# 16 products of zeros ahead of the first sums in place of 21

## The chip, the core and the metric

One core of one Trainium2 chip. The metric is the device time of one execution in microseconds; the time of a kernel is the median of its runs. Five engines work side by side, each through its own instructions in order: TensorE (PE; its weight loads are listed apart as PEld), VectorE (DVE), ScalarE (ACT), GpSimd (POOL) and SyncE (SP), which here only issues DMAs.

## What is computed

A gated linear recurrence over 768 steps for 4 x 8 heads of width 48, and behind it a two-layer network with the gate h * cos(h):

```python
for t in range(S):
    state = alpha[:, :, t, :, None] * state + np.einsum('bhd,bhe->bhde', k[:, :, t], v[:, :, t])
    y[:, :, t] = np.einsum('bhd,bhde->bhe', q[:, :, t], state)
...
h = x @ w_in
g = h * np.cos(h)
return (g @ w_out).astype(np.float32)
```

x is y with the heads of a step side by side: 3072 rows of 384; w_in is 384 x 2048, w_out 2048 x 384.

## The kernel before

The 3072 rows are cut into 12 pairs J of two blocks of 128 steps. Each pair goes through the same steps:

- `load` (L105, SP's queue): alpha, k, q and v of the pair, 384 KB each. `load_w1` and `load_w2` (L121, L127) bring the weights in four pieces each, issued by POOL.
- `ln` (L141, ACT): logarithms of alpha, tile lna.
- `cums0` and `cums` (sums at L155, decay sums at L167, PE): running sums of the logarithms by products with triangular matrices, tile cums_h for the first three pairs.
- `icp` and `exps` (L192, L200, ACT): exponentials of the sums with both signs, tiles icp and cp.
- `scale_k` (L212) and `scale_q` (L216), on DVE or POOL: kh = k * icp and qh = q * cp. `cast_v` (L219, POOL) makes vp of v, `decay` (L244, POOL) the factors c.
- `outer` (L291, PE): the state's increments U_ps from kh and vp. `stack_v_pe` (L235, PE, pairs 0 to 2) regroups v through vs_ps, and ACT copies it to vs (L239). `trans` (L260, PE) turns kh and qh into T_ps, `evict_T` (L266) copies that to qkT.
- `scores` (L274, PE) gives A_ps, `mask` (L279, DVE) A_sb; `add_state` (L305, L307, DVE) and `decay_state` (L313, POOL) carry the state on as us and un.
- `yT` (L340, PE) gives y_ps, `evict_y` (L350) xT. Then `mlp1` (L359, PE, tile h_ps, four parts a pair), `cosine` (L365, ACT, c_sb), `gate` (L370, DVE, gsb) and `mlp2` (L387, PE, o_ps), whose result `evict_o` (L396) copies out and `store` (L403) writes.

The order is written out by hand. `PLAN` gives a due time in ns for each step of each pair, and the steps are emitted in the order of these numbers; the numbers do not become waits. Each engine then runs its own instructions in that order, and waits only for its data and buffers. Two loads have a further condition: from pair 2 on, alpha is gated behind `yT` of pair 1 on SP's queue (`GATES`, L99), with all that SP issues after it.

`idle(n)` (L407 to L411) puts n products of a 128x128 tile of zeros with a 128x512 tile of zeros on PE. Their result, idle_ps, is never read. Their only input is the tile zeros, which DVE's first instruction sets (L52). `IDLE` (L494) says where they stand among the steps, as pairs of due time and number. The first entry lies ahead of all sums; one product follows the sums of pair 0, eight those of pair 1, and the other four entries lie between the next steps up to 18,254.

Of the kernel before, what the change touches and what calls it, by code (L numbers as in the profile page):

```python
# [16 lines left out]
def kernel(  # L17
# [473 lines left out]
        "out 0": "47770 53670 76970 97327 92197 114044 134921 150722 154222 155552 167028 178835",  # L491
        "out 1": "44770 66136 87674 100827 112274 133721 136121 156752 149522 168228 170958 180161",
    }
    IDLE = [(1501, 21), (7915, 1), (9416, 8), (12569, 4), (14554, 5), (16389, 3), (18254, 3)]  # L494

    order = []
    for key, line in PLAN.items():
        kind, *rest = key.split()
        for J, word in enumerate(line.split()):
            if word != "-":  # L500
                t, _, eng = word.partition(":")
                args = [J] + [int(x) if x.isdigit() else x for x in rest] + [{"A": "ACT", "D": "DVE", "P": "POOL"}[x] for x in eng]
                order.append((int(t), len(order), kind, args))
    for t, n in IDLE:
        order.append((t, len(order), "idle", [n]))
# [34 lines left out]
```

## Time and profile before

| | |
|---|---|
| median of 3 runs | 190.49 us (189.67, 190.49, 190.68) |
| profiled execution | 189.73 us, of which the span from its first to its last instruction is 187.7 us |
| PE busy | 177.2 us, 94% of the span |
| DVE, ACT, POOL busy | 72%, 67%, 41% of the span |
| products of zeros (L411) | 42 listed, 12.7 us busy |
| first sums (L155) | start at 8.03 us |

Times in the profile count from the start of the span. In a timeline a row gives the start, the duration, the engine, the line, the operation, the tiles written and read, and how many such instructions follow one another; what stands in brackets is the idle time of the engine before the row and what ended it. Matmuls overlap, so the distance from one start to the next tells more of PE's pace than the duration of one. Some products are missing from the lists.

### The profile page before, as it was taken

What the parts mean: (1) busy time and instruction counts of PE and PEld (TensorE: products, weight loads), DVE (VectorE), ACT (ScalarE), POOL (GpSimd) and SP (SyncE); (2) the same over time, 40 slices, a digit from 0 to 9 for tenths busy, and PEclk for the clock granted to TensorE, in tenths of its full rate; (3) what the DMA queues carried; (4) which work ended last, traced back from release to release, by engine and by line L of the source; (5) the groups of instructions that cost most, each with busy time, mean ns of one, the idle gap of its engine ahead of it and who ended that gap; (6) DMA issues with size and microseconds to landing.
All of it is one profiled execution on the core that took longest, in us unless ns stands there. A gap on an engine that the chain in (4) does not pass through costs nothing.

```text
span 187.7 us, 5795 instructions
## 1 busy us (share of the span) xinstructions
PE 177.2 (94%) x2471; PEld 126.7 (67%) x2474; DVE 134.3 (72%) x184; ACT 125.3 (67%) x161; POOL 77.4 (41%) x110
## 2 busy tenths in 40 slices
PE   7997799998999999999999999999999999999990
PEld 2444678664577776775688668686776786776880
DVE  7069775589799899589657986885876666573550
ACT  2466876899598977788577999728956182372520
POOL 5059610257664733783894068830540310100000
PEclk9999999999999999999999999999999999999998
DMA  6999999999959988996799943600042005501303
GB/s 152 261 256 154 185 203 236 255 264 265 249 137 302 265 184 217 265 268 166 195 280 259 216 106 90 166 0 3 3 114 73 0 21 124 128 1 45 84 0 84
DMA packets 60537, 29.47 MB, mean 157 GB/s; under 512 B 51424, under 2 KB 60512, under 8 KB 60512
## 3 DMA queue, kind: packets, MB, share of 16 engines
q1 hardware_dynamic: 56640, 25.86, 59.8%
q0 software_dynamic: 3712, 3.15, 11.0%
q8 instruction: 19, 0.31, 0.7%
q10 hardware_dynamic: 160, 0.10, 0.2%
q14 instruction: 6, 0.05, 0.1%
HBM read 25.17 MB, written 4.72 MB: 159 GB/s over the span
## 4 chain that ended last, share of the span: by engine, by line
PE 71%; ACT 16%; DVE 7%; issue 3%; DVEq 0%
PE h_ps L359 31%; PE o_ps L387 23%; PE idle_ps L411 5%; PE y_ps L340 3%; ACT c_sb L365 3%; ACT qkT L266 3%; DVE gsb L370 3%; PE T_ps L260 2%; ACT cp L200 2%; ACT L136 2%; ACT L365 2%; PE A_ps L274 2%; PE U_ps L291 2%; ACT lna L141 2%; ACT icp L192 2%
## 5 line engine op out<-in xcount | busy, mean ns | idle before, releaser
L370 DVE TENSOR_TENSOR gsb<-h_ps,c_sb 128x1024 bf16<-128x1024 f32 x48 | 58.1, 1221 | 22.3 <-ACT c_sb L365 21.5
L365 ACT ACTIVATE c_sb<-h_ps,halfpi 128x1024 bf16<-128x1024 f32 x48 | 53.0, 1113 | 27.4 <-PE h_ps L359 23.4
L359 PE MATMUL h_ps<-xT,w 128*128 128x256 bf16 x576 | 66.7, 273 | 1.4 <-issue 0.6
L387 PE MATMUL o_ps<-w,gsb 128*128 128x384 bf16 x368 | 66.7, 326 | 0.0
L359 PEld LDWEIGHTS <-w 128*128 128x128 bf16 x576 | 55.6, 98 | 10.4 <-issue 1.9
L387 PEld LDWEIGHTS <-gsb 128*128 128x128 bf16 x368 | 33.8, 98 | 21.2 <-DVE gsb L370 0.6
L313 POOL TENSOR_TENSOR un<-us,c 128x384 bf16<-128x384 f32 x20 | 16.8, 843 | 40.3 <-DVE us L305 33.9
L279 DVE TENSOR_TENSOR A_sb<-A_ps,msk 128x1024 bf16<-128x1024 f32 x24 | 28.9, 1216 | 1.3 <-PE A_ps L274 1.3
L212 POOL TENSOR_TENSOR kh<-k,icp 128x384 bf16<-128x384 f32 x17 | 16.9, 999 | 8.7 <-ACT icp L192 8.7
L216 POOL TENSOR_TENSOR qh<-q,cp 128x384 bf16<-128x384 f32 x15 | 15.4, 1032 | 10.9 <-ACT cp L200 10.9
L149 POOL TENSOR_TENSOR a<-a 128x384 f32<-128x384 f32 x9 | 9.3, 1037 | 12.9 <-DMA a<-in_alpha_dram 12.9
L411 PE MATMUL idle_ps<-zeros 128*128 128x512 bf16 x42 | 12.7, 445 | 1.6 <-DVE zeros L52 1.2
L219 POOL CAST vp<-v 128x768 bf16<-128x768 f32 x12 | 9.9, 824 | 9.0 <-DMA v<-in_v_dram 8.9
L141 ACT ACTIVATE lna<-a 128x768 bf16<-128x768 f32 x12 | 10.2, 846 | 4.5 <-DMA a<-in_alpha_dram 4.5
L136 ACT ACT_TABLE_LOAD x9 | 11.5, 1283 | 0.9 <-PEq L524 0.7
L266 ACT COPY qkT<-T_ps 128x1024 bf16<-128x1024 bf16 x8 | 8.0, 1016 | 6.2 <-PE T_ps L260 3.8
L266 DVE COPY qkT<-T_ps 128x1024 bf16<-128x1024 bf16 x16 | 10.8, 682 | 1.3 <-ACT qkT L266 1.3
L365 ACT ACT_TABLE_LOAD x9 | 11.5, 1283 | 0.2
L305 DVE TENSOR_TENSOR us<-U_ps,un 128x384 f32<-128x384 f32 x16 | 8.7, 550 | 3.8 <-PE U_ps L291 2.8
L396 DVE COPY o_sb<-o_ps 128x384 f32<-128x384 f32 x12 | 6.6, 552 | 6.6 <-PE o_ps L387 6.6
L274 PE MATMUL A_ps<-qkT 48*128 48x128 bf16 x192 | 9.2, 218 | 1.0 <-ACT vs L239 0.6
L396 ACT COPY o_sb<-o_ps 128x384 f32<-128x384 f32 x11 | 5.3, 478 | 7.1 <-PE o_ps L387 5.2
(69 smaller groups left out, 155.1 us busy)
## 6 DMA issues: line engine op xcount, KB each, us to landing
k<-in_k_dram SPq DMA_DIRECT2D x12, 384.0 KB, 5.5
a<-in_alpha_dram SPq DMA_DIRECT2D x12, 384.0 KB, 5.9
v<-in_v_dram SPq DMA_DIRECT2D x12, 384.0 KB, 6.2
q<-in_q_dram SPq DMA_DIRECT2D x12, 384.0 KB, 6.0
out_dram<-o_sb SPq DMA_DIRECT2D x46, 96.0 KB, 2.7
vs<-vp SPq DMA_DIRECT2D x36, 64.0 KB, 2.0
w<-in_moe_w_out_dram POOLq DMA_DIRECT2D x4, 384.0 KB, 9.9
w<-in_moe_w_in_dram POOLq DMA_DIRECT2D x4, 384.0 KB, 7.0
```

The costliest lines, as they stand in the source:

```text
L136: nc.scalar.preload_act_table_set("natural_log_exp_and_others")
L141: nc.scalar.activation(out=lna_t[J % NL][:, :, :, 0:D].rearrange("p e h d -> p h e d"), in_=a_sb.pop(J), func=AF.Ln)
L212: eng.tensor_tensor(out=kh_t[J % NQ][:, e, :, 0:D], in0=kqv["k", J][:, :, e], in1=icp_, op=ALU.mult)
L216: eng.tensor_tensor(out=qh_t[J % NQ][:, e, :, 0:D], in0=kqv["q", J][:, :, e], in1=cp, op=ALU.mult)
L266: copy(out=qkT_sb[J][:, c], in_=T_ps[J][:, c].rearrange("r n e s -> r n (e s)"))
L279: nc.vector.tensor_tensor(out=A_sb[J][:, c].rearrange("s a p t -> s (a p) t"), in0=A_ps.pop((J, c)).rearrange("s a p t -> s (a p) t"), in1 ...
L313: nc.gpsimd.tensor_tensor(out=u, in0=U_sum.pop(n), in1=c2_sb[J][:, :, c].unsqueeze(3).to_broadcast([C, NP, 2, D]), op=ALU.mult)
L359: nc.tensor.matmul(h_ps[J, u][:, f, :], w1[:, kk, ft * C : (ft + 1) * C], xT[J][:, kk, :], start=(kk == 0), stop=(kk == KT - 1))
L365: nc.scalar.activation(out=c_sb[J, u], in_=h_ps[J, u], func=AF.Sin, bias=halfpi, scale=1.0)
L370: nc.vector.tensor_tensor(out=gsb[J][:, u * FW : (u + 1) * FW], in0=h_ps.pop((J, u)), in1=c_sb.pop((J, u)), op=ALU.mult)
L387: nc.tensor.matmul(o_ps[J, c][:, 0:DM], gsb[J][:, ft, c * C : (c + 1) * C], w2[:, ft], start=(ft == 0), stop=(ft == NF - 1))
L411: nc.tensor.matmul(idle_ps[0], zeros[:, 0:C], zeros, start=True, stop=True)
```

## The change

The first entry of `IDLE` holds 16 in place of 21. Its place among the steps stays, and no other step is touched.

```diff
-    IDLE = [(1501, 21), (7915, 1), (9416, 8), (12569, 4), (14554, 5), (16389, 3), (18254, 3)]
+    IDLE = [(1501, 16), (7915, 1), (9416, 8), (12569, 4), (14554, 5), (16389, 3), (18254, 3)]
```

On PE five pairs of a weight load and a product go; the order of all else, on PE and on the other engines, is the same.

## Prediction

> **What bounds the kernel now.** I read the page first, then the chain that ended last in order of time, then the timelines of the first 24 us, because the change touches only there.
>
> The page:
>
> ```profile
> span 187.7 us, 5795 instructions
> ...
> PE 177.2 (94%) x2471; PEld 126.7 (67%) x2474; DVE 134.3 (72%) x184; ACT 125.3 (67%) x161; POOL 77.4 (41%) x110
> ```
>
> PE is busy 94% of the span, so what PE starts earlier at the front may be kept to the end, if nothing stops it on the way. The chain, in order of time (start, us, what), says whether the front is PE's:
>
> ```profile
> 1.20 7.00 PE idle_ps L411 x21
> 8.19 0.65 PE cums_h L155 x4
> 8.84 0.18 PE cums_h L167 x8
> 9.02 0.24 PE idle_ps L411
> 9.26 0.65 PE cums_h L155 x4
> 9.91 0.19 PE cums_h L167 x8
> ...
> 11.03 1.10 DVE kh L212 x2
> ...
> 12.18 0.47 PE U_ps L291 x14
> 12.65 0.30 PE vs_ps L235 x4
> 12.95 0.97 PE idle_ps L411 x4
> 13.92 0.59 PE T_ps L260 x32
> ```
>
> The 21 products of zeros head the chain, and the chain never leaves the instructions behind them: sums of pair 0, sums of pair 1, ACT's exponentials, DVE's kh, then PE again. What did the first sums need? ACT's timeline:
>
> ```profile
> 5.86 0.84 ACT L141 ACTIVATE lna<-a 128x768 bf16<-128x768 f32 x1 [3.83 <-DMA a<-in_alpha_dram]
> 7.36 0.84 ACT L141 ACTIVATE lna<-a 128x768 bf16<-128x768 f32 x1 [0.67 <-DMA a<-in_alpha_dram]
> 9.06 0.49 ACT L192 ACTIVATE icp<-cums_h 128x384 f32<-128x384 f32 x1 [0.85 <-PE cums_h L167]
> ```
>
> The logarithms of pair 0 end at 6.70 (5.86 + 0.84), those of pair 1 at 8.20. PE starts the first sums only at 8.03 (PE's timeline), 1.33 us after their input: the zeros, not the data, hold them. ACT then stands idle 0.85 us, from 8.20 to 9.06.
>
> **The change, step by step.** The instruction order differs in five weight loads and five products of zeros on PE; no wait, no DMA and no other engine's order changes.
>
> Step 1, the removed products. PE's weight loads, one for each product, give the spacing:
>
> ```profile
> 5.01 0.15 PEld L411 LDWEIGHTS <-zeros 128*128 128x128 bf16 x1 [0.28 <-issue]
> 5.44 0.15 PEld L411 LDWEIGHTS <-zeros 128*128 128x128 bf16 x1 [0.28 <-issue]
> 5.86 1.84 PEld L411 LDWEIGHTS <-zeros 128*128 128x128 bf16 x9 [0.28 <-issue]
> 7.82 0.10 PEld L155 LDWEIGHTS <-tri 128*128 128x128 bf16 x1
> ```
>
> One product each 0.43 us up to 5.86, then nine loads in 1.84 us: (1.84 - 0.10) / 8 = 0.217 us each. The column of the granted clock says 1.00 all the while; that the array runs at half rate until about 5.9 us is seen in the spacing alone. The five products taken out are behind that point (single starts: the 12th at 5.86, the 17th at 6.95, the 21st at 7.82). So the first sums move from 8.03 to 6.95, by 5 x 0.217 = 1.08 us. Their input is there at 6.70, so nothing new is late.
>
> Step 2, the sums of pair 1. They stood at 9.10, and would go to 8.02. Their logarithms end at 8.20; PE followed such a row by 0.06 us later in the trace (Ln ends 36.84, PE 36.90). They start at about 8.25: **0.85 us** earlier, and 0.23 of the 1.08 are lost to ACT. ACT's first exponential goes from 9.06 to 8.21, so ACT's seven exponentials, which run without a gap from 10.13 on, also move by 0.85.
>
> Step 3, what lies beside them. DVE's kh follows ACT. The k inputs landed at about 4.3 (issue 0.74 + 3.6) and 8.9 (2.87 + 6.0), in time. U_ps also needs the cast of v, and that is tied to a DMA and does not move: it ends at 11.24. The kh that U_ps waits for ended at 12.13 and would end at 11.28. A tie, so no loss by the cast's end; but now DVE's kh run beside it. The timeline of all engines shows what such neighbours did:
>
> ```profile
> 10.42 0.82 POOL L219 CAST vp<-v 128x768 bf16<-128x768 f32 x1 [7.23 <-DMA v<-in_v_dram]
> ...
> 11.03 1.56 DVE L212 TENSOR_TENSOR kh<-k,icp 128x384 bf16<-128x384 f32 x3 [0.89 <-ACT icp L192]
> ...
> 12.96 1.03 DVE L216 TENSOR_TENSOR qh<-q,cp 128x384 bf16<-128x384 f32 x2 [0.37 <-ACT cp L200]
> ...
> 14.37 1.66 DVE L216 TENSOR_TENSOR qh<-q,cp 128x384 bf16<-128x384 f32 x2
> ...
> 14.61 1.01 POOL L313 TENSOR_TENSOR un<-us,c 128x384 bf16<-128x384 f32 x1
> ```
>
> Two qh alone took 1.03 us; two beside POOL's un took 1.66. Taken singly, the second of these took 1.19 in place of 0.55, a loss of 0.64, beside a POOL product that reads two tensors. The only row beside this cast is the first kh, at 11.03: 0.62 in place of 0.55, with 0.21 us in common, a loss of 0.06. After the change some 0.8 us of kh lies beside the cast. The bounds are 0.06 and 0.64; going by the row of the cast itself, 0.06 / 0.21 x 0.82 = 0.23, I take **0.20**. U_ps thus moves by 0.85 - 0.20 = 0.65.
>
> The GPSIMD Engine Reference of the Trainium skill (section Specifications) says that GpSimd shares its SBUF interfaces with VectorE and contends with DVE instructions that have two SBUF inputs, as kh has. The qh rows agree. By that rule alone, with no price, this step costs something; with no contention the sum would be 0.85.
>
> Step 4, behind U_ps. vs_ps, four products of zeros and T_ps follow without a gap on PE, and ACT's copy at 14.54 had waited 1.61 us for T_ps; they move with U_ps. qh of pair 0 would start at 12.11 (12.96 - 0.85); q landed at about 11.8 by the 1.5 us steps of the loads (a at 5.86 and 7.36, the second q at 7.09 + 6.2 = 13.3). Enough. qh of pair 1 goes from 14.37 to 13.52, against 13.3.
>
> Step 5, the weights, which could eat the gain. POOL issues them behind the same exponentials (c at 12.24 waits for ACT), so they are issued earlier too. Even if they landed as before, they would do: the second block of w1 lands at 22.26 (15.56 + 6.7) and is used at 23.7; the third at 24.33 (17.13 + 7.2), used at 25.04; the fourth at 26.8 (17.91 + 8.9), used at 27.49. The smallest slack is 0.69, over the 0.65. The next alpha, gated by yT of pair 1, landed at 34.66 and was used at 36.00. From 28 us on everything waits for PE, ACT or DVE, and moves as a whole.
>
> **The sum**: -1.08 + 0.23 + 0.20 = -0.65 us. Against the profiled execution, 189.73 us (span 187.7 and 2.03 around it), that gives 189.08. The three timed runs have their median at 190.49, 0.76 above the profiled one; taken from the median, **189.84 us**, or -0.34%. About 0.5% (0.95 us) is what a measurement of this kernel can tell from no change.
>
> **The rivals.**
>
> *Late release.* The Trainium skill, TensorE: Matmul & The Clock Gate (Part 1), says that the window which frees the clock runs freely, so that the number of slow products differs from execution to execution. No view here shows a second execution. As a mechanism of this kernel: each product still slow costs 0.43 - 0.22 = 0.21 us more, and 0.76 us, the distance of the median from the profiled run, are 3.6 such products. Then the 21 end at about 8.8 and the 16 at about 7.7; pair 1's logarithms hold nothing back, and the full 1.08 is kept but for some 0.1 beside the cast (kh would start near 10.7, when half of the cast is over). 190.49 - 0.98 = 189.51. For it: the runs differ by 1.0 us. Against: the spread may have other causes. Chance 0.27.
>
> *The cast at its full price.* If a kh beside the cast loses 0.64, as beside un, 0.21 us are left: 190.28. Against it: the cast reads one tensor, and its own row is far cheaper. Chance 0.15.
>
> *Slower: the clock falls back.* With five products fewer, PE has its next hole earlier and larger: the eight products behind pair 1's sums would end at about 10.83, and U_ps starts at 11.5, a hole of some 0.65 us where now there is 0.1 (last zeros issued 11.46, U_ps at 11.77) and then 0.19. If a hole of that size in the weakly filled stretch from 11 us on were enough to halve the rate again, the next release would take as long as the first, 1.20 to 5.86, that is 4.66 us. PE's pieces of the chain in 11.5 to 16.2 are U_ps, vs_ps, zeros and T_ps, 0.47 + 0.30 + 0.97 + 0.59 = 2.33 us, and they double: -0.65 + 2.33 = +1.68, 192.2 us. The point is a hole longer than any seen without harm: PE stood 0.62 us before 16.30 and 0.50 before 22.25, and products of zeros just behind the first still took 0.22. That speaks against it. Chance 0.13.
>
> That the change does not do what it says is excluded by the instruction order.
>
> **Chances and range.** Forecast 0.45, late release 0.27, full price 0.15, clock 0.13. The range 189.0 to 191.0 holds the first three with a spread of half a microsecond in the median, and leaves out the slow clock. Faster by over 0.5% means under 189.54: half of the late release, with the lower edge of the forecast (no contention gives 189.64), and part of the runs' spread: 0.34. Slower by over 0.5% is the clock: 0.13. Within: 0.53.
>
> **What would show it.** Step 1: first sums near 6.95, weight loads of zeros 0.43 apart up to about 5.9. Step 2: pair 1's sums just behind the end of the second Ln, ACT's first exponential at 8.2. Step 3: DVE's kh at about 10.2 and longer than 0.55; U_ps at 11.5. Step 5: first h_ps near 21.6, with no wait for weights. Wrong: products at 0.43 us after 11 us, or h_ps earlier by 0.65 and the span not.

## The result, and the profile after

The changed kernel takes 189.09 us in the median of 10 runs (188.69 to 189.64), the kernel before 190.50 (189.64 to 190.78): a ratio of 0.9939, with a 95% interval of 0.9918 to 0.9961. Two later comparisons of the same two kernels (below) gave 0.9964 (0.9944 to 0.9983) and 0.9954 (0.9933 to 0.9976). The gain is thus some 0.4% to 0.6%, 0.7 to 1.2 us; 0.34% was forecast.

The profiled executions show less of it: 189.54 us against 189.73.

```profile
span 187.5 us, 5788 instructions
...
PE 176.4 (94%) x2469; PEld 126.2 (67%) x2469; DVE 134.8 (72%) x184; ACT 125.3 (67%) x161; POOL 77.8 (42%) x110
```

The first sums and ACT's first exponential start within 0.1 us of the forecast, pair 1's sums 0.16 later. The timeline of all engines of the changed kernel (start, duration, engine, line, operation):

```profile
6.01 0.84 ACT L141 ACTIVATE lna<-a 128x768 bf16<-128x768 f32 x1 [3.99 <-DMA a<-in_alpha_dram]
...
6.91 0.32 PE L155 MATMUL cums_h<-lna,tri 128*128 128x384 bf16 x1 [0.40 <-ACT lna L141]
...
7.52 0.84 ACT L141 ACTIVATE lna<-a 128x768 bf16<-128x768 f32 x1 [0.66 <-DMA a<-in_alpha_dram]
...
8.27 0.47 ACT L192 ACTIVATE icp<-cums_h 128x384 f32<-128x384 f32 x1
8.41 0.32 PE L155 MATMUL cums_h<-lna,tri 128*128 128x384 bf16 x1 [0.28 <-ACT lna L141]
...
10.34 2.14 DVE L212 TENSOR_TENSOR kh<-k,icp 128x384 bf16<-128x384 f32 x3 [1.01 <-ACT icp L192]
10.56 1.02 POOL L219 CAST vp<-v 128x768 bf16<-128x768 f32 x1 [7.38 <-DMA v<-in_v_dram]
```

The first sums start at 6.91, the moment their logarithms are there, those of pair 1 at 8.41 in place of 9.10; ACT no longer waits at 8.3. Then the gain is lost: three kh take 2.14 us in place of 1.56, for the second, which starts at 10.82 inside POOL's cast, takes 1.18 in place of 0.55. The chain of the changed kernel, in order of time, carries the loss on:

```profile
8.41 0.81 PE cums_h L155 x4
9.22 0.19 PE cums_h L167 x8
...
10.34 1.66 DVE kh L212 x2
...
12.05 0.47 PE U_ps L291 x14
...
13.78 0.59 PE T_ps L260 x32
...
22.11 2.79 PE h_ps L359 x24
```

U_ps comes at 12.05 against 12.18, and the first h_ps at 22.11 against 22.25. That is this line of the kernel before:

```profile
22.25 2.79 PE h_ps L359 x24
```

The front, moved by 0.7 us at pair 1's sums, gave 0.14.

Nor was the zeros' pace the same. PE's weight loads of the changed kernel:

```profile
4.16 0.15 PEld L411 LDWEIGHTS <-zeros 128*128 128x128 bf16 x1 [0.27 <-issue]
4.58 1.43 PEld L411 LDWEIGHTS <-zeros 128*128 128x128 bf16 x7 [0.28 <-issue]
6.13 0.10 PEld L155 LDWEIGHTS <-tri 128*128 128x128 bf16 x1
```

The fast spacing begins at 4.58, where before it began at 5.86.

The largest difference between the two traces lies far behind the front. The chain of the kernel before, and then that of the changed one, in the 72 h_ps products of 95 to 104 us:

```profile
95.46 2.84 PE h_ps L359 x25
98.30 0.62 issue
98.92 5.31 PE h_ps L359 x47
```

```profile
95.77 3.38 PE h_ps L359 x30
99.15 0.12 issue
99.27 4.76 PE h_ps L359 x42
```

PE stands 0.62 us behind the 25th product and waits for nothing that the profile shows; with five pairs of instructions fewer it stands 0.12 us behind the 30th. Counted in PE's weight loads and products from the first one, it is the same place, row 2737: the block begins at row 2687 before and at 2677 after (three products of zeros that the list of before lacks are counted in, since their weight loads are listed). The block as a whole takes 8.77 us before and 8.26 after.

### The profile page after: what moved, and what is told of

Its sections match the earlier page's. It is cut to its first block, busy times and chain, and to the rows that moved or that the text cites. A ratio compares the mean times of both kernels' runs of the same rounds, so it can differ in the third digit from the quotient of the medians.

```text
span 187.5 us, 5788 instructions
## 1 busy us (share of the span) xinstructions
PE 176.4 (94%) x2469; PEld 126.2 (67%) x2469; DVE 134.8 (72%) x184; ACT 125.3 (67%) x161; POOL 77.8 (42%) x110
## 4 chain that ended last, share of the span: by engine, by line
PE 57%; ACT 16%; DVE 7%; DMA 6%; POOL 5%; SPq 4%; issue 3%; POOLq 0%; DVEq 0%
PE h_ps L359 25%; PE o_ps L387 20%; ACT c_sb L365 4%; PE y_ps L340 3%; DMA a<-in_alpha_dram 3%; DMA v<-in_v_dram 3%; ACT qkT L266 3%; DVE gsb L370 3%; ACT L136 2%; SPq L225 2%; PE T_ps L260 2%; ACT L365 2%; PE A_ps L274 2%; ACT icp L192 2%; ACT cp L200 2%
## 5 line engine op out<-in xcount | busy, mean ns | idle before, releaser
L411 PE MATMUL idle_ps<-zeros 128*128 128x512 bf16 x40 | 11.5, 431 | 1.2 <-DVE zeros L52 1.2
```

## The experiments

The theory from here on is in two parts. **Front**: the first sums are freed, and how much of that reaches U_ps hangs on the release of the clock and on kh beside the cast. **Refill**: the hole is a wait for PE's next packet of instructions, and five pairs fewer shift where among the h_ps it lies. The rival to each is that the other is all.

This table gathers what the traces show, one profiled execution each, in us: begin of the fast spacing, start of the 14 products of U_ps that wait for the second of two kh, start of the first h_ps, length of the 72 h_ps of 95 to 104 us and the hole in it with the product it follows, and the ratio to the kernel before with its interval.

| kernel | fast from | U_ps | h_ps | block, hole | ratio |
|---|---|---|---|---|---|
| before (21) | 5.86 | 12.18 | 22.25 | 8.77, 0.62 at 25 | |
| changed (16) | 4.58 | 12.05 | 22.11 | 8.26, 0.12 at 30 | 0.9939 (0.9918 to 0.9961) |
| e1, 21 again | 4.98 | 12.21 | 22.26 | 8.73, 0.59 at 25 | 0.9999 (0.9978 to 1.0021) |
| e2, 16 again | 6.29 | 12.00 | 22.05 | 8.19, 0.05 at 30 | 0.9964 (0.9944 to 0.9983) |
| e3, 21, v first | 4.54 | 11.59 | 21.65 | 8.43, 0.29 at 25 | 0.9982 (0.9956 to 1.0008) |
| e4, 16, v first | 6.29 | 11.54 | 21.59 | 7.98, none | 0.9928 (0.9903 to 0.9953) |
| e5, 16 + 5 tiny | 4.16 | 12.12 | 22.17 | 8.32, 0.18 at 25 | 0.9983 (0.9962 to 1.0003) |
| e6, 21, 5 fewer later | 6.66 | 12.46 | 22.60 | 8.00, none | 0.9978 (0.9951 to 1.0004) |
| e7, 26 | 4.97 | 12.72 | 22.85 | 9.49, 1.35 at 20 | 1.0084 (1.0054 to 1.0114) |
| e8, 5 moved | 5.01 | 12.42 | 22.47 | 8.94, 0.80 at 25 | 0.9992 (0.9975 to 1.0009) |
| e9, 11 | 4.07 | 12.11 | 22.16 | 8.71, 0.57 at 35 | 0.9950 (0.9927 to 0.9974) |
| e10, 16 a third time | 6.71 | 12.16 | 22.21 | 8.02, none | 0.9954 (0.9933 to 0.9976) |

**Second profiles of both kernels** (no edit).

> The kernel before, unchanged, for a second profile. Front theory (the gain is made ahead of 22 us, and its size in one execution hangs on when the clock is released and on what DVE's kh meet beside POOL's cast): the release of the clock, seen in the spacing of the zeros' weight loads, lies elsewhere than at 5.9 us, and each slow product more delays the first sums by 0.21 us; with a release 1.5 us later the sums start near 8.8 and the time is near 190.6, with the same release near 189.8. Rival (the gain is made in a later stage): the first h_ps starts near 22.25 whatever the time of the execution, and a slower execution loses its time behind 40 us.

Measured: 190.04 us in the median. The release came 0.9 us earlier, and pair 1's sums with it (strict's weights at 8.64 in place of 9.10). U_ps did not. PE's weight loads of e1, and then its DVE timeline:

```profile
4.98 2.26 PEld L411 LDWEIGHTS <-zeros 128*128 128x128 bf16 x11 [0.24 <-issue]
7.36 0.10 PEld L155 LDWEIGHTS <-tri 128*128 128x128 bf16 x1
```

```profile
10.57 2.06 DVE L212 TENSOR_TENSOR kh<-k,icp 128x384 bf16<-128x384 f32 x3 [0.89 <-ACT icp L192]
```

With 21 products too, an early release puts the kh beside the cast, and three take 2.06 us: U_ps comes at 12.21. That was not expected; it means that with an early release 21 and 16 products reach U_ps within about 0.2 us of each other.

> The changed kernel, unchanged, for a second profile. Front theory: first sums at 6.9 to 7.1; where the second kh takes 0.55 us the first h_ps starts near 21.5 and the time is near 188.8, where it takes 1.18 as in the first profile h_ps starts near 22.1 and the time is near 189.5. Rival: first h_ps near 22.1 in both cases, and the difference arises behind it.

Measured: 189.46 us. The second kh was slow again (three in 2.14 us), and h_ps came at 22.05, as expected for that case. The profiled execution, at 189.22, was 0.3 faster than the first, with h_ps only 0.06 earlier; the rest arose between 78 and 89 us, so the rival's remark on a later stage was right.

**The cast out of the way**: v of pair 0 is loaded ahead of k of pair 1, with 21 products (e3) and with 16 (e4).

```diff
-        "load v": "3750 8250 ...
+        "load v": "2300 8250 ...
```

> 21 products, and v of pair 0 loaded ahead of k of pair 1, so that POOL's cast ends near 9.8, ahead of the kh. Front theory: with 21 products the cast lay hardly beside the kh (0.06 us), so this gives 190.4, within 0.2 of the kernel before. Rival: the order of these two loads does not matter with 21 nor with 16.

Measured: 190.09. As expected in time; in its trace, with an early release, three kh took 1.50 us and h_ps came 0.6 earlier. That execution, at 188.84, was the fastest of the twelve, so its trace does not stand for their median.

> 16 products, and the same exchange of two loads. Front theory: the cast is off the kh, each of the three takes 0.55 us, U_ps starts near 11.5 in every execution, h_ps near 21.5, and the time is 188.8 with less spread, 0.3 to 0.5 below the median of 16 products alone; against 21 products with the same exchange 1.0 to 1.6 us are won. Rival: within 0.2 us of 16 products alone (189.1).

Measured: 188.85, a ratio of 0.9928, as the front theory had it; by the quotient of the two ratios 16 products win 0.5% over 21 here (1.0 us). Less spread was not seen: six runs lie between 188.19 and 189.34. DVE's timeline of e4:

```profile
10.45 1.50 DVE L212 TENSOR_TENSOR kh<-k,icp 128x384 bf16<-128x384 f32 x3 [1.15 <-DMA k<-in_k_dram]
```

The cast ends ahead of them, each takes 0.55 again, and U_ps is 0.5 us ahead of 16 products alone. So in the traces of 16 the front's gain was lost beside the cast, and 0.5 us of it can be had. With v first, k lands later and the kh wait for it, with 21 as with 16: U_ps comes at 11.59 and at 11.54. The 1.0 us is thus not in the front of these two executions: they differ by 0.55 us, of which 0.45 lies in the block of h_ps. What more the medians differ by, no trace shows. By its median, e4 is the fastest kernel here; its interval overlaps that of 16 products alone.

**The refill.** In e5 five products of two columns stand ahead of the first h_ps, so that PE's rows from there on are counted as with 21; in e6 the 21 stay, and five of the eight products behind pair 1's sums go, so that the rows from U_ps on are counted as with 16.

```diff
+            nc.tensor.matmul(idle_ps[0][:, 0:2], zeros[:, 0:C], zeros[:, 0:2], start=True, stop=True)
...
+    order.append((21900, len(order), "tiny", [5]))
```

```diff
-    IDLE = [(1501, 21), (7915, 1), (9416, 8), ...
+    IDLE = [(1501, 21), (7915, 1), (9416, 3), ...
```

> 16 products ahead of the first sums, and five products of two columns of zeros just ahead of the first h_ps, where PE waits 0.5 us for ACT anyway; from there on PE's instructions are counted as with 21. Refill theory (a part of the gain is that PE's next packet of instructions, needed at its row 2737, comes into the h_ps of 95 to 104 us five products later than with 21): the hole behind the 25th of these 72 products is back, 0.3 to 0.6 us, where with 16 it is 0.05 to 0.12 behind the 30th; the time is about 0.5 above 16 products alone, near 189.8. Front theory alone: no hole of its own, the time of 16 products, 189.1 to 189.5.

> 21 products ahead of the first sums, and three in place of eight behind the sums of pair 1, where PE waits for kh anyway; from U_ps on PE's instructions are counted as with 16. Refill theory: front as with 21 (U_ps' second product at 12.2 or later, h_ps at 22.25 or later), but the hole is behind the 30th product of the h_ps of 95 to 104 us and under 0.2 us; the time lies 0.5 below the kernel before, near 189.7. Front theory alone: the time of the kernel before, 190.1, as the sums are where they were. If the clock falls back in the hole ahead of U_ps, slower by over 1 us.

Measured: 189.74 and 189.51. The chain of e5, then that of e6, over the same products:

```profile
95.42 2.83 PE h_ps L359 x25
98.26 0.18 issue
98.44 5.31 PE h_ps L359 x47
```

```profile
95.81 8.00 PE h_ps L359 x72
```

The hole is back at the 25th product with 16 zeros in front, smaller than expected, and gone with 21. So its place hangs on how many instructions precede it and not on the front. Its length hangs on the packet too: in e5 a packet on the queue "q8 instruction" moved at 95.70, in the kernel before at 96.14, with the block at 95.42 and at 95.46. Each of the two kernels has about one half of the gain (0.2% each). Their intervals reach 1, so the times alone do not prove the halves; the traces show that the hole comes and goes with the count. In e6 PE stood 0.82 us ahead of those 14 products of U_ps, longer than any hole of the changed kernel there (0.49), and the next four products of zeros were as fast as before (four weight loads in 0.55 us).

**Five more, and five moved.**

```diff
-    IDLE = [(1501, 21), (7915, 1), ...
+    IDLE = [(1501, 26), (7915, 1), ...
```

> 26 products ahead of the first sums. Front theory: the sums start 1.08 later than with 21 at the same release of the clock; up to a release near 5 us the cast's place beside the kh is left at the same time, so that U_ps moves by 0.4 to 0.5 then, and by 1.08 with a later release: 0.5 to 1.1 slower than the kernel before. Refill theory adds 0.3 to 0.5, as the hole comes behind the 20th product: 0.8 to 1.5 slower in all, 191.0 to 191.6.

Measured: 191.58, a ratio of 1.0084; between the bounds. U_ps came 0.54 later and h_ps 0.60, with an early release, and the hole grew to 1.35 us behind the 20th product. The chain of e7:

```profile
96.07 2.29 PE h_ps L359 x20
98.36 1.35 issue
99.71 5.85 PE h_ps L359 x52
```

```diff
-    IDLE = [(1501, 16), (7915, 1), ...
+    IDLE = [(1501, 16), (7915, 6), ...
```

> 16 products ahead of the sums of pair 0, and the other five moved behind them, ahead of the sums of pair 1. Front theory: the chain goes over pair 1, whose sums start near 9.0 as with 21 and an early release; with a late release they are 0.2 to 0.5 later than with 16. Refill theory: as many instructions as with 21, so the hole of 0.6 us near 98 us is there. Both: 190.0, hardly under the kernel before. If the sums of pair 0 carried the gain: 189.4.

Measured: 189.96, a ratio of 0.9992. Pair 0's sums started as early as with 16 and brought nothing: the front goes over pair 1, and the hole (0.80 us) is back behind the 25th product, as with 21.

**Fewer still, and 16 a third time.**

```diff
-    IDLE = [(1501, 16), ...
+    IDLE = [(1501, 11), ...
```

> 11 products ahead of the first sums, five fewer again. Both theories: the sums wait for the logarithms as with 16, so U_ps stays near 12.0; the hole near 98 us would lie behind the 35th product and is gone, 0 to 0.1 us less than with 16: 189.0 to 189.4. If the clock needs the zeros: they end near 5.5, PE stands until 6.9, and in executions where the clock is not yet released the sums of both pairs take twice as long (0.8 us each in place of 0.4 to 0.5): up to 1 us slower than 16, with more spread.

> The changed kernel a third time, for its ratio beside 11 products on one chip. Front and refill together: 0.4% to 0.6% under the kernel before; first h_ps near 22.1, a hole of 0 to 0.15 us behind the 30th product of the h_ps of 95 to 104 us.

Measured: 188.91 and 189.36, ratios of 0.9950 and 0.9954. Eleven are no better than 16, as the sums wait for the logarithms in both, and U_ps for the cast: in the five executions with 16 or 11 products and v in its old place, U_ps starts 1.49 to 1.51 us behind the start of the cast, which waits for v's load. Nor was the clock lost: in this execution, with 11, PE stood 1.85 us ahead of the first sums, and the four took 0.81 us, as in the first trace with 16:

```profile
6.94 0.32 PE L155 MATMUL cums_h<-lna,tri 128*128 128x384 bf16 x1 [1.85 <-ACT lna L141]
```

The profiled execution of e9 took 191.12 us; the other ten lie at 188.8 to 189.8. It shows a third place that gives and takes: POOL's cast of v that waits for its load near 77 us. That load was issued at 72.49 by SP behind slow issues of regrouping DMAs (4.47 us for four, 3.53 in e2); what follows came 1.1 us later than in the first trace of 16. The packet moved at 98.85, 2.0 us behind the start of the h_ps at 96.87 in place of 0.3 to 0.9 in the other traces, and the hole, 0.57 us behind the 35th product, was there all the same. "Gone" was too much to expect.

## Why the prediction was right, and where it was not

*Steps 1 and 2* held: first sums at 6.91 (forecast 6.95), pair 1's at 8.41 (8.25, with the logarithms themselves 0.16 later), ACT's first exponential at 8.27 (8.21). That the first sums hit 6.95 is luck: with the fast spacing from 4.58 the zeros were through earlier, PE stood 0.40 us, and the logarithms, not the zeros, set the 6.91.

*Step 3* is the term that was mis-sized. The mechanism, kh beside the cast, was named and bounded between 0.06 and 0.64; the value taken was 0.20, and the two kh ahead of U_ps took 1.66 us in place of 1.10, which is 0.56. What failed is the scaling of the loss with the time in common (0.06 / 0.21 x 0.82). The rows show a wait instead. These are single kh of the changed kernel, of e1 and of e8, and behind the last two the cast that each met:

```profile
10.82 1.18 DVE L212 TENSOR_TENSOR kh<-k,icp 128x384 bf16<-128x384 f32 x1
```

```profile
10.57 1.11 DVE L212 TENSOR_TENSOR kh<-k,icp 128x384 bf16<-128x384 f32 x1 [0.89 <-ACT icp L192]
...
10.45 0.82 POOL L219 CAST vp<-v 128x768 bf16<-128x768 f32 x1 [7.26 <-DMA v<-in_v_dram]
```

```profile
11.08 0.82 DVE L212 TENSOR_TENSOR kh<-k,icp 128x384 bf16<-128x384 f32 x1 [1.65 <-ACT icp L192]
...
10.66 0.82 POOL L219 CAST vp<-v 128x768 bf16<-128x768 f32 x1 [7.47 <-DMA v<-in_v_dram]
```

The casts end at 11.58, 11.27 and 11.48, the kh at 12.00, 11.68 and 11.90: each 0.41 to 0.42 behind the cast, however long the two ran side by side. The kernel before fits (11.65 behind 11.24), and so does its second qh behind un (16.03 behind 15.62). So the prediction's two bounds, 0.06 and 0.64, were one behaviour, met late or early in POOL's instruction. It works the other way too: a cast that starts while a kh runs ends 0.68 behind that kh (11.58 behind 10.90 in the changed kernel, 10.13 behind 9.45 in e3), and the kh, having come first, loses nothing (0.56). With 0.56 the step would have left 0.85 - 0.56 = 0.29 at U_ps; the logarithms came 0.16 later in this execution, and 0.13 was measured. The GPSIMD Engine Reference of the Trainium skill (section Specifications) has it that DVE instructions with two SBUF inputs contend with GpSimd. These rows agree; the price is theirs alone.

*Steps 4 and 5* held: T_ps and the copies moved with U_ps, no h_ps waited for weights. The sentence that from 28 us on everything moves as a whole did not. It holds to 78 us, where the changed kernel is 0.14 ahead. At 89 us it is 0.3 behind, since the cast of v at 77 us waited longer for its load; behind the h_ps of 95 to 104 it is 0.20 ahead, for that block takes 0.51 less. The refill was in no term and in no rival, though the hole stood in the page's chain as "issue" and could be found there.

*The rivals.* Late release: the release does differ from execution to execution, from 4.07 to 6.71 us in twelve traces, as the Trainium skill, TensorE: Matmul & The Clock Gate (Part 1), has it. With 16 products the logarithms cover that: U_ps comes at 12.00 to 12.16 with a release at 4.58 as at 6.71. With 21 it costs: e6, released at 6.66, has U_ps at 12.46, 0.25 to 0.28 behind the two with 5.86 and 4.98. So in such executions 16 products gain 0.30 to 0.46 us at U_ps, against 0.02 to 0.21 in the others, and this rival is probably a part of the median's gain; how large a part is not shown, as the traces do not say how often a late release comes. No trace caught one as late as the 7.4 us that the rival's 0.98 needs (3.6 slow products of 0.43 behind 5.86). The cast at its full price: its 0.64 is what the second kh lost (0.63); for the two together it is 0.56, since the first, which had lost 0.06 before, now came ahead of the cast and lost nothing. The clock that falls back: not in any trace, with holes of 0.49 and 0.20 us ahead of U_ps with 16, up to 0.82 there in e6, and 1.85 us ahead of the first sums in e9.

So it is luck that the forecast's 0.65 us lies near the measured 0.7 to 1.2. It was reached by terms that offset each other: in an execution with an early release the front gave about 0.5 us less than forecast, and the h_ps block gave about 0.5 that was not forecast; what late releases add is argued and not shown.

Open: why a packet comes when it does. The queue named "q8 instruction" moves 19 packets, 0.31 MB, in a run in which PE has about 4,950 rows; that it carries PE's instructions is inferred. In the kernel before a packet moves at 96.14 us, and the hole ends at 98.92; 96.37 and 98.91 in e1, 96.56 and 99.27 in the changed kernel, 96.87 and 99.71 in e7. In all nine traces with a hole it ends 2.5 to 2.8 us behind the packet, and in the three without one PE came to the row 2.6 to 2.7 us behind it. That the hole is the wait for this packet is inferred from the fixed row and this distance; it was not tried with the DMAs taken away.

## What to carry to other kernels

Follow a freed engine to the next instruction that it brings beside another engine's work. Before scaling a loss with the time in common, compare several rows: if the instruction that came second always ends at the same distance behind the first, it waits, and its price is what the first had left to run. Removing or adding instructions, even idle ones, can shift where among PE's later instructions such a hole lies, so look for "issue" holes in the long blocks and count instructions up to them before calling a later stage unmoved. And one profiled execution shows one release of the clock: where the first products run at half rate, compare several traces before giving the front a price.

## What the runs showed of the hardware that was not expected

- A DVE product of two tensors in SBUF that started inside POOL's cast ended 0.41 to 0.42 us behind the cast's end, whenever it had started: it took 0.62, 0.82, 1.11 and 1.18 us in place of 0.55. A cast that started inside such a product ended 0.68 us behind the product's end (1.02 and 1.17 us in place of 0.82).
- PE stood 0.05 to 1.35 us at one fixed row of its instructions (2737), the hole ending 2.5 to 2.8 us behind a packet on the instruction queue, in nine of twelve executions. With fewer instructions ahead of that row, so that it came later in the block, it mostly stood less or not at all.
- The half rate at the start ended between 4.07 and 6.71 us of the span in twelve executions, while the column of the granted clock read 1.00 throughout.
